# Attention with normalized queries and keys, then a gated feed-forward: repeats of the rest queries on VectorE or GpSimd, k and v of pairs 2 to 5 in runs of three tokens, score steps two at a time

## The chip, the cores and the metric

The kernel runs on one core of a Trainium2 chip. The metric is the device time of one execution in microseconds; before the change it is 424.69 (median of 3 runs, 423.41 to 424.93). The core has five engines with instruction queues of their own: TensorE (PE), VectorE (DVE), ScalarE (ACT), GpSimd (POOL) and SyncE (SP), and 16 DMA engines that serve the queues of SP, ACT and POOL.

## The reference

Eight batches of twelve heads, 448 tokens, 64 elements a head. Queries and keys are normalized, softmax attention is computed, the heads of a token are put side by side, and two matrix products with a gate between them follow.

```python
rms = np.sqrt(np.mean(x * x, axis=-1, keepdims=True) + 1e-06)   # for q and for k
...
scores = scale * np.matmul(q_n, k_n.transpose(0, 1, 3, 2))
attn = np.exp(scores - max); attn = attn / (sum(attn) + 1e-09)
x = np.matmul(attn, v).transpose(0, 2, 1, 3).reshape(3584, 768)
h = x @ w_in                                  # 768 x 2048
g = h * np.clip(h + 3.0, 0.0, 6.0) / 6.0
out = g @ w_out                               # 2048 x 768
```

## The kernel before

**Tiling.** Two heads make a pair; there are 48 pairs, six to a batch. The 448 tokens of a head are three full tiles of 128 and a rest of 64. A pair's work is: load k, q and v (`load_main`, `load_rest`), square (`square`, L403 on GpSimd or L401 on ScalarE), sum (`sums`, L406 on VectorE), the reciprocal root (`rstd`, L417 and L419 on ScalarE), normalize into bf16 (`normalize`, L427 and L429), turn tokens by elements into elements by tokens (`transposes` on TensorE up to pair 11, a DMA transpose from pair 12 on: `TD`), copy out of PSUM with the product of the two gains multiplied into the queries (`put_k`, and `put_q`, L465 on ScalarE or L467 on VectorE), four score steps (`score`, L476), four exponentials (`expo`, L492, or `expo_head`, L497), four weighings of v (`weigh`, L513), a division by the row sums (`divide`, L523 to L532), and a transpose back (`x_out`, L541 to L547, or a DMA).

**Score steps.** Step 0, 1 and 2 of a pair take one full tile of keys each, with two half-height matmuls (64 rows, one for each head) into two PSUM banks; step NT = 3 takes the rests of both heads in one full-height matmul. `steps(todo)` makes a chain of several steps that TensorE runs in a row. Pairs under `PB` go one step at a time, pairs up to `P3` two at a time, from `P3` on three at a time. Single and double steps write banks 0 and 1 (two halves each). A group of three puts its first step in banks 2 and 3 (`THIRD`), which the feed-forward uses otherwise, and its exponentials are those of L497. In the tile eR of a rest step `expo` writes 448 columns and, in a second small exponential, once more the last 64 at column 512 (`W4`), from where the weighing of the second head's rest reads them.

**Two orders of tokens.** The first `PD = MB = 6` pairs (batch 0) are dense: partition s of a half holds seven neighbouring tokens, so that q and k come in one run of 1792 bytes for each partition, with no separate rest; v comes in two transfers, one for each half of the partitions, with a rest of its own. Dense tiles are transposed in 64 x 64 pieces. Later pairs hold three neighbouring tokens on each of 128 partitions and load the rest of 64 tokens apart, beside zeros that `clear` writes. The weights arrive through GpSimd's queue in pieces (`W_IN`).

**Feed-forward.** `h_mm` (L561) makes 128 columns of h for a batch from six matmuls, `relu` (L567, ScalarE) and `gate` (L572, VectorE) make g, `y_mm` (L580) makes 128 tokens by 384 outputs from sixteen matmuls. They are the items of the lanes "h" and "y", take one of the banks that `FF` lists, and run on TensorE between the steps of the attention. Batch 0's first h column may begin when pair 4's output is there (`h_early`), the others when all six are.

**What sets the order.** The class `Plan` simulates the engines while the program is built, and writes the instructions out in the order that comes of it: `key` ranks an operation, `ways` lists the engines that may take it with an estimated duration, and the prices `FIRST` (up to 45 us) and `PRICE` (after it) weigh one engine against another. Every engine runs its instructions in the written order, so one that waits holds up all behind it. `hold(p)` puts a small write on GpSimd behind the normalization of pair p - 5 (p under 12) or p - `LA`; the loads of pair p wait for it. The product of the gains goes through `load_g`, `mix_g` (VectorE), `turn_g` (a matmul) and `put_g` (VectorE, L639). `DN` lists the normalizations that VectorE does (L427, of pairs 0 and 1), the others are GpSimd's.

## Time and profile before

| what | value |
|---|---|
| median of 3 runs | 424.69 us (423.41 to 424.93) |
| the profiled execution | 423.99 us, its span 422.1 us |
| granted TensorE clock over the span | 1.0 |
| ScalarE, VectorE, GpSimd busy | 291.7, 210.6, 201.3 us |
| moved by DMA | 65.12 MB, mean 154 GB/s |
| batch 0's last output transposes (pair 5) | from 39.23 us on TensorE |
| last exponential of the attention | ends before 320 us; GpSimd's last work before 300 us |

The page gives busy times of each engine, the chain of work that ended last, and groups of instructions by line. A view of windows gives the same for stretches of the span, the timeline lists instructions in order of their start, with the idle time before them and what ended it in brackets. On TensorE matmuls overlap: the duration of a row is longer than the step to the next start, and the distance of two starts is what a matmul costs. "x4" behind a row counts the instructions merged in it.

### The profile page before, as it was taken

Reading aid. Unit: us, or ns where it says so; the run is one execution under the profiler, and the core shown is the slowest. Engines: PE = TensorE matmul, PEld = TensorE weight load, DVE = VectorE, ACT = ScalarE, POOL = GpSimd, SP = SyncE. Lnnn points to the kernel's source line nnn. Section 1 sums busy time; section 2 is a strip of 40 time slices with the busy share of each in tenths; the row PEclk is TensorE's granted clock in tenths of the full one; section 3 lists DMA queues with packets and bytes.
Section 4 is the critical chain, followed back from the end, with each engine's and each line's share of the span. In section 5 each row is a group of like instructions: output and inputs, shape, how many; then the busy total and the mean of one; then the engine's idle time right before and its main releaser. Section 6 shows DMA issues by size and latency. Waiting matters only on the chain.

```text
span 422.1 us, 9498 instructions
## 1 busy us (share of the span) xinstructions
PE 406.6 (96%) x3692; PEld 237.1 (56%) x3692; DVE 210.6 (50%) x436; ACT 291.7 (69%) x713; POOL 201.3 (48%) x215
## 2 busy tenths in 40 slices
PE   2989999999999999999999999999999999999997
PEld 1565655455555555555555556565556555555565
DVE  7775978455444676457364664546243152042100
ACT  5899986766888988897869977789583243243211
POOL 5998956747676647756575676681000000000000
PEclk9999999999999999999999999999999999999999
DMA  8999899999998959988896968943420301100122
GB/s 253 252 217 235 155 235 176 198 244 176 189 246 208 245 109 201 233 195 202 158 248 168 248 122 198 255 106 77 76 64 13 88 0 39 75 2 37 76 75 76
DMA packets 124561, 65.12 MB, mean 154 GB/s; under 512 B 77412, under 2 KB 121060, under 8 KB 124516
## 3 DMA queue, kind: packets, MB, share of 16 engines
q1 hardware_dynamic: 116144, 57.76, 61.2%
q0 software_dynamic: 8080, 6.29, 10.2%
q8 instruction: 29, 0.48, 0.5%
q10 hardware_dynamic: 292, 0.46, 0.3%
q14 instruction: 16, 0.13, 0.1%
HBM read 45.61 MB, written 11.01 MB: 134 GB/s over the span
## 4 chain that ended last, share of the span: by engine, by line
PE 81%; ACT 5%; DMA 5%; issue 2%; DVE 2%; POOL 2%; SPq 1%; POOLq 0%; DVEq 0%; ACTq 0%
PE ps L580 34%; PE ps L561 29%; PE av L513 9%; PE sc L476 6%; DMA v_st<-in_v_dram 3%; ACT eD L492 3%; DMA qkT<-qkn 2%; PE ps L476 1%; DMA qk_st<-in_q_dram 1%; POOL qkn L429 1%; DVE ssq L406 1%; ACT t_sb L567 1%; PE ps L446 1%; SPq L376 1%; PE sc L561 1%
## 5 line engine op out<-in xcount | busy, mean ns | idle before, releaser
L561 PE MATMUL ps<-xT,w_in_sb 128*128 128x448 bf16 x750 | 165.4, 352 | 1.5 <-ACT eD L497 1.1
L580 PE MATMUL ps<-w_out_sb,gT 128*128 128x384 bf16 (+1 forms) x896 | 162.5, 323 | 0.0
L572 DVE SCALAR_TENSOR_TENSOR gT<-t_sb,ps 128x448 bf16<-128x448 f32 x125 | 76.9, 620 | 110.5 <-ACT t_sb L567 109.6
L492 ACT ACTIVATE eD<-sc 128x768 bf16<-128x768 f32 x240 | 113.3, 567 | 6.0 <-PE sc L476 5.6
L580 PEld LDWEIGHTS <-gT 128*128 128x128 bf16 x912 | 83.8, 98 | 57.2 <-issue 8.8
L561 PEld LDWEIGHTS <-w_in_sb 128*128 128x128 bf16 x768 | 69.8, 98 | 57.6 <-issue 6.1
L429 POOL TENSOR_TENSOR qkn<-qk_st,rstd 128x512 bf16<-128x512 f32 x84 | 85.2, 1043 | 25.0 <-ACT rstd L419 24.7
L403 POOL TENSOR_TENSOR sq<-qk_st 128x1024 f32<-128x1024 f32 (+2 forms) x50 | 81.6, 1642 | 31.8 <-DMA qk_st<-in_q_dram 18.5
L567 ACT ACTIVATE t_sb<-ps 128x448 f32<-128x448 f32 x125 | 69.8, 562 | 31.1 <-PE ps L561 28.5
L513 PEld LDWEIGHTS <-eD 128*128 128x128 bf16 x1152 | 52.4, 98 | 23.2 <-issue 6.3
L406 DVE TENSOR_REDUCE ssq<-sq 128x16 f32<-128x1024 f32 (+2 forms) x50 | 57.7, 1156 | 8.9 <-POOL sq L403 5.9
L379 ACT COPY y_sb<-ps 128x384 f32<-128x384 f32 (+1 forms) x43 | 20.6, 478 | 57.4 <-PE ps L580 57.3
L513 PE MATMUL av<-vaug,eD 128*128 128x65 bf16 x1152 | 58.9, 194 | 0.0
L476 PE MATMUL sc<-qkT 64*128 64x448 bf16 (+1 forms) x288 | 52.8, 358 | 3.2 <-DVE qkT L467 1.1
L379 POOL CAST vaug<-v_st 128x512 bf16<-128x512 f32 x29 | 17.7, 620 | 39.2 <-PE av L513 38.7
L497 ACT ACTIVATE eD<-ps 128x448 bf16<-128x448 f32 (+2 forms) x72 | 25.1, 419 | 15.7 <-PE ps L476 15.7
L492 ACT ACTIVATE eR<-sc 128x448 bf16<-128x448 f32 x96 | 32.9, 412 | 3.1 <-PE sc L476 2.9
L523 DVE RECIPROCAL rden<-av 128x7 f32<-128x7 f32 x48 | 9.7, 202 | 40.4 <-PE av L513 40.2
L476 PEld LDWEIGHTS <-qkT 64*128 64x128 bf16 (+1 forms) x336 | 15.4, 95 | 22.2 <-issue 14.5
L465 ACT ACTIVATE qkT<-qkT,gprime 128x448 bf16<-128x448 bf16 x36 | 24.8, 691 | 1.7 <-DMA qkT<-qkn 1.7
L529 DVE TENSOR_TENSOR xn<-av,rden 128x384 bf16<-128x384 f32 x42 | 23.4, 557 | 1.5
L513 PEld LDWEIGHTS <-eR 128*128 128x128 bf16 x240 | 16.7, 99 | 7.2 <-issue 1.9
(72 smaller groups left out, 177.8 us busy)
## 6 DMA issues: line engine op xcount, KB each, us to landing
qk_st<-in_k_dram SPq DMA_DIRECT2D x21, 384.0 KB, 4.0
qk_st<-in_q_dram SPq DMA_DIRECT2D x21, 384.0 KB, 5.5
v_st<-in_v_dram SPq DMA_DIRECT2D x21, 384.0 KB, 5.9
out_dram<-y_sb SPq DMA_DIRECT2D x20, 384.0 KB, 2.4
w_out_sb<-in_moe_w_out_dram POOLq DMA_DIRECT2D x4, 768.0 KB, 11.1
out_dram<-y_sb SPq DMA_DIRECT2D x15, 192.0 KB, 2.7
w_in_sb<-in_moe_w_in_dram POOLq DMA_DIRECT2D x3, 768.0 KB, 9.5
v_st<-in_v_dram SPq DMA_DIRECT2D x22, 64.0 KB, 5.7
```

The lines of the kernel that those rows point to most:

```text
L379: (eng.copy if eng is nc.scalar else eng.tensor_copy)(out=out, in_=in_)
L403: eng.tensor_tensor(out=sq, in0=x, in1=x, op=A_MULT)
L406: nc.vector.tensor_reduce(out=packed(p, ssq_r[:, p % NR, a]), in_=packed(p, sq_r[m % 2][:, a]), axis=mybir.AxisListType.X, op=A_ADD,)
L429: eng.tensor_tensor(out=qkn_r[p % NQ][:, a].rearrange("p t h d -> p h t d"), in0=qk_st[:, a, p % NS], in1=by[:, a].rearrange("p (h t) -> p ...
L476: nc.tensor.matmul(out=(bank(u[h]) if isinstance(u, tuple) else bank(u, h))[:, 0:S], lhsT=qkT[rows, 0, i * P:(i + 1) * P], rhs=qkT[rows, 1 ...
L492: nc.scalar.activation(out=out, in_=in_, func=EXP, bias=0.0, scale=1.0)
L497: nc.scalar.activation(out=e[:, c:c + cols.stop - cols.start], in_=src[:, cols], func=EXP, bias=0.0, scale=1.0)
L513: nc.tensor.matmul(out=av_ps[:, c:c + n], lhsT=e_part(p, i, h, j), rhs=va[:, i].rearrange("p h d -> p (h d)")[:, h * W:h * W + n], start=f ...
L561: nc.tensor.matmul(out=bank(m)[:, 0:S], lhsT=w_in_sb[:, kt, f * P:(f + 1) * P], rhs=xT[:, kt, b % NX, x_slot(b)], start=(kt == 0), stop=(k ...
L567: nc.scalar.activation(out=t[:], in_=bank(m)[:, 0:S], func=RELU, bias=0.5, scale=1.0 / 6.0,)
L572: nc.vector.scalar_tensor_tensor(out=gT[:, f, (b % 2) * S:(b % 2 + 1) * S], in0=t[:], scalar=1.0, in1=bank(m)[:, 0:S], op0=A_MIN, op1=A_MULT,)
L580: nc.tensor.matmul(out=bank(m)[:, 0:n], lhsT=gT[:, f, c0:c0 + P], rhs=w_out_sb[:, f, c:c + n], start=(f == 0), stop=(f == NFT - 1),)
```

## The change

- **Repeats.** The second, small exponential of a rest step goes. A new function `repeat` copies the 64 columns inside eR, on VectorE or GpSimd as the plan chooses.
- **Score steps.** `P3` becomes 48, so no group of three is left; `PB` becomes 10. The feed-forward's list of banks becomes (2,), (3,), (4,), with banks 0 and 1 added after the last score.
- **k and v of pairs 2 to 5.** A new constant `PK = 2` beside `PD = 6`: `is_dense(a, p)` is true for q up to pair 5, for k and v up to pair 1. k and v of pairs 2 to 5 come in runs of three tokens with rests apart; `clear` splits into `clear_k` and `clear_q`, and the unused eighth block of squares is cleared once.
- **Gains.** `mix_g` is a plain product on GpSimd and waits for the sums of pair 0 instead of its normalized values; the factor 1/8 moves into `unit`.
- **Pair 1.** `DN` keeps pair 0 alone, so pair 1 is normalized on GpSimd. The key of a normalization becomes (.., 4).
- **Constants.** Prices and estimates of the plan; `NQ` 4 for 5; `XQ` 4 for 6 (pairs whose output is packed in seven blocks and transposed by five matmuls); `TS` 6 for 12 (pairs from 6 on turn k and q into one bank); `LA` 4 for 3, with p - 4 for p under 10 in `hold`; `W_IN` in six pieces; the order of the first loads.

```diff
-    PRICE, FIRST, UNTIL = {"POOL": 0.5, "ACT": 1.5, "DVE": 1.5}, {"POOL": 0.5, "ACT": 1.7, "DVE": 1.0}, 45e3
+    PRICE, FIRST, UNTIL = {"POOL": 0.6, "ACT": 2.0, "DVE": 1.2}, {"POOL": 0.7, "ACT": 1.2, "DVE": 1.0}, 45e3
...
-    NV, NK, NX, NQ, NR = 4, 3, 3, 5, 4
+    NV, NK, NX, NQ, NR = 4, 3, 3, 4, 4
...
-    W_IN = 512, 256, 256, 512, 512
+    W_IN = 256, 256, 256, 256, 512, 512
...
-    TD, XD, XQ = 12, 12, 6
+    TD, XD, XQ = 12, 12, 4
...
-    DENSE, PD, MB = 2 * NT + 1, 6, 6
+    DENSE, PK, PD = 2 * NT + 1, 2, 6
...
+    def is_dense(a, p):
+
+        return p < (PK, PD, PK)[a]
...
-        if a < 2 and p < PD:
+        if a < 2 and is_dense(a, p):
...
-        if p < MB:
+        if is_dense(a, p):
             src = src.rearrange("h (s r) d -> s h (r d)", r=DENSE)
             for u, part in enumerate((lo, hi)):
...
+    def blocks(p, a):
+
+        return DENSE if all(is_dense(i, p) for i in range(a.start, a.stop)) else 8
...
         if i == NT:
             e, src = eR_t[:, p % NER], bank(u)
-            parts = (e[:, 0:S], src[:, 0:S]), (e[:, W4:W4 + REST], src[:, FULL:S])
+            parts = ((e[:, 0:S], src[:, 0:S]),)
...
+    def repeat(eng, p):
+
+        e = eR_t[:, p % NER]
+        eng.tensor_copy(out=e[:, W4:W4 + REST], in_=e[:, FULL:S])
...
-    def clear(eng, r):
+    def clear_k(eng, r):
         eng.memset(qk_st[REST:P, 0, r, 0, NT, :], 0.0)
         eng.memset(qk_st[0:REST, 0, r, 1, NT, :], 0.0)
+
+    def clear_q(eng, r):
         eng.memset(qk_st[REST:P, 1, r, :, NT, :], 0.0)
...
-        eng.memset(unit[:], 1.0)
+        for sq in sq_r:
+            eng.memset(sq[:, 1, DENSE:8], 0.0)
+        eng.memset(unit[:], 1.0 / 8.0)
...
-    def mix_g():
-
-        nc.vector.scalar_tensor_tensor(
-            out=g_two[:], in0=g_row[:, 0:1].to_broadcast([1, 2, D]), scalar=1.0 / 8.0,
-            in1=g_row[:, 1:2].to_broadcast([1, 2, D]), op0=A_MULT, op1=A_MULT,
-        )
+    def mix_g(eng):
+
+        eng.tensor_tensor(out=g_two[:], in0=g_row[:, 0:1].to_broadcast([1, 2, D]), in1=g_row[:, 1:2].to_broadcast([1, 2, D]), op=A_MULT)
...
-    SC, ANY = [(0,), (1,)], [(2,), (3,), (4,), (1,), (0,)]
+    SC, ANY = [(0,), (1,)], [(1,), (0,), (4,), (3,), (2,)]
...
-    FF = [(3,), (2,), (4,), (1,), (0,)], [(4,)]
+    FF = [(2,), (3,), (4,)], [(4,)]
...
-    W_AFTER, LA, VL = 2, 3, 1.2
-    DN = ((0, 0), (0, 1), (1, 0), (1, 1))
+    W_AFTER, LA, VL = 2, 4, 1.2
+    DN = ((0, 0), (0, 1))
...
-    V0, V2, LATER, AHEAD = 2.5, 0.8, -1, 2500
+    V0, V2, LATER, AHEAD = 2.5, 0.8, -1, 4000
...
-        held[p] = [add((-5, p), [("POOL", 80, lambda: nc.gpsimd.memset(cell, 0.0))], norms[p - (5 if p < 12 else LA)] + norms.get(p - NS, []))]
+        held[p] = [add((0, p), [("POOL", 80, lambda: nc.gpsimd.memset(cell, 0.0))], norms[p - (4 if p < 10 else LA)] + norms.get(p - NS, []))]
...
-    TS, WAIT = 12, True
+    TS, WAIT = 6, True
...
-            load(1, 1, 1, 0, 0, nc.scalar, "ACT")
-            lg = plan.dma((0.5, 1), 2, 40, lambda: load_g(nc.scalar), queue="ACT")
+            load(1, 1, 1, 0, 0, *Q1)
+            lg = plan.dma((0, 1.5), 2, 40, lambda: load_g(nc.scalar), queue="ACT")
...
-            load(0, 2, 2, 2 * (PD <= 2), 0)
-            load(1, 2, 2, 2 * (PD <= 2), 0)
-            load(2, 0, 2, 4, V0)
-            lv = load(2, 2, 2, 0, 2.5)
+            load(0, 2, 2, 4 * (PK <= 2), 0)
+            load(1, 2, 2, 0, 0)
+            load(2, 0, 2, 2, 2.0)
+            lv = load(2, 2, 2, 4, 0.3)
...
-            m1 = add((-3, 0), [("DVE", 450, mix_g)], [lg, *norms[0]])
+            m1 = add((-3, 0), [("POOL", 330, lambda: mix_g(G))], [lg, squares[0]])
...
-                    e = [add((p, 0), [("ACT", 850 if i < NT else 545, lambda p=p, i=i, c=cells[n]: expo(p, i, c["b"]))], [ops[n], old])]
+                    e = [add((p, 0), [("ACT", 850 if i < NT else 440, lambda p=p, i=i, c=cells[n]: expo(p, i, c["b"]))], [ops[n], old])]
                     (op.parts[n - 1] if third else op.gives).append(e[0])
+                    if i == NT:
+                        e.append(by((p, 0.5), 160, 100, lambda eng, p=p: repeat(eng, p), e))
...
-            PB, P3 = 8, 24
+            PB, P3 = 10, 48
```

More of the change, by code (lines that the diff above doesn't have):

```diff
@@ L204, in run @@
                     continue
-                if op.calm is not None and (self.backlog("SP", "ACT") > op.calm[0] + 0 or self.backlog("POOL") > op.calm[1]):
+                if op.calm is not None and (self.backlog("SP", "ACT") > op.calm[0] + 500 or self.backlog("POOL") > op.calm[1]):
                     continue
@@ L330, in bank16 @@
         return bank(u).bitcast(BF16)
[L332 removed]
+    plan = Plan(share=(2.0, 1.0, 0.45, 3.0, 0.42, 6.0, 0.4))
     add = plan.add
@@ L441, in transposes @@
     def transposes(p, b, which=range(2)):
-        for a in which if p < PD else ():
+        for a in (a for a in which if is_dense(a, p)):
             for t in range(DENSE):
@@ L449, in transposes @@
                 nc.tensor.transpose(bank16(b)[part, c0:c0 + D], none[part, :], identity[part, part])
-        for a in which if p >= PD else ():
+        for a in (a for a in which if not is_dense(a, p)):
             for t in range(4):
@@ L834, in stats @@
         else:
-            s2 = [add((st, 3), [("DVE", 1000 if p < PD else 1130, lambda: sums(p, both, m))], s1 + busy)]
+            s2 = [add((st, 3), [("DVE", 1000 if p < PK else 1130, lambda: sums(p, both, m))], s1 + busy + [zero])]
         squares.append(s2[-1])
```

103 lines of the change are left out of this document (55 added, 48 removed).

## The prediction

> **What bounds the kernel now.** I read the page first: engine times, then DMA queues.
>
> ```profile
> span 422.1 us, 9498 instructions
> PE 406.6 (96%) x3692; PEld 237.1 (56%) x3692; DVE 210.6 (50%) x436; ACT 291.7 (69%) x713; POOL 201.3 (48%) x215
> q1 hardware_dynamic: 116144, 57.76, 61.2%
> ```
>
> TensorE is the bound, with 15.5 us of the span idle. The execution took 423.99 us, so 1.9 us lie around its span; it is 0.7 us (0.16%) below the median of the runs, 424.69, and inside their spread. All sums below start from 423.99.
>
> Second, the view of windows: length, busy time and (count) of PE, PEld, DVE, ACT and POOL, granted clock, DMA share, GB/s.
>
> ```profile
> 20.00:36.00 16.00, 14.61 (x237) 9.69 (x236) 10.86 (x24) 15.70 (x44) 15.76 (x23) 1.00 1.12 230
> 80.00:160.00 80.00, 80.00 (x726) 44.63 (x725) 43.25 (x85) 64.66 (x152) 50.15 (x48) 1.00 1.03 206
> 160.00:320.00 160.00, 158.50 (x1494) 92.28 (x1493) 84.16 (x172) 132.01 (x337) 88.83 (x85) 1.00 0.77 165
> ```
>
> There are two regimes. From 20 to 36 us ScalarE (15.70 of 16.00) and GpSimd (15.76) are full, VectorE is not (10.86), and TensorE has only attention to do, since the feed-forward of batch 0 needs the outputs of its six pairs. There a microsecond taken from the leading chain moves everything after it. From 80 us on TensorE always has feed-forward matmuls beside the attention: no idle time from 80 to 160, where pairs are scored two steps at a time, and 160.00 - 158.50 = 1.5 us from 160 to 320, where most pairs are scored three at a time. There only matmul time and waits for a PSUM bank count; work taken from ScalarE is worth nothing by itself.
>
> **Score steps.** The chain of waits gives TensorE's undisturbed pace (start, length, line, count): 12.48 / 66 = 0.189 us for an input matmul, 8.78 / 54 = 0.163 for an output one.
>
> ```profile
> 324.57 8.78 PE ps L580 x54
> 333.34 12.48 PE ps L561 x66
> ```
>
> The timeline of TensorE then prices a group of steps:
>
> ```profile
> 105.22 0.73 PE L561 MATMUL ps<-xT,w_in_sb 128*128 128x448 bf16 x3
> 105.88 0.55 PE L476 MATMUL sc<-qkT 64*128 64x448 bf16 x4
> 106.37 0.42 PE L513 MATMUL av<-vaug,eD 128*128 128x65 bf16 x8
> ```
>
> ```profile
> 204.85 2.27 PE L580 MATMUL ps<-w_out_sb,gT 128*128 128x384 bf16 x13
> 207.05 0.36 PE L476 MATMUL ps<-qkT 64*128 64x448 bf16 x2
> 207.25 0.54 PE L476 MATMUL sc<-qkT 64*128 64x448 bf16 x4
> 207.73 0.34 PE L580 MATMUL ps<-w_out_sb,gT 128*128 128x384 bf16 x1
> ```
>
> ```profile
> 36.53 0.36 PE L476 MATMUL sc<-qkT 64*128 64x448 bf16 x2
> 36.82 0.36 PE L561 MATMUL ps<-xT,w_in_sb 128*128 128x448 bf16 x1
> ```
>
> Two steps cost 106.37 - 105.22 - 3 x 0.189 = 0.58 us, of which 105.88 - 105.22 - 0.57 = 0.09 is the entry from full-height matmuls. Three cost 207.73 - 204.85 - 13 x 0.163 = 0.77. One costs 36.82 - 36.53 plus that entry, 0.38 to 0.39. So pairs 24 to 47 pay 1.5 x 0.58 - 0.77 = 0.10 us each when triples go: **+2.4 us**. PB from 8 to 10 turns the three double groups of pairs 8 and 9 into six single ones: 6 x 0.39 - 3 x 0.58 = **+0.6 us**. Both lie in stages where TensorE is the bound, so nothing hides them.
>
> Against that stand the waits. A triple takes two of the three banks that the feed-forward asks for first, and the ends of the two largest waits between 160 and 320 us are:
>
> ```profile
> 185.18 1.11 PE L561 MATMUL ps<-xT,w_in_sb 128*128 128x448 bf16 x5 [0.85 <-ACT eD L497]
> 311.52 0.73 PE L561 MATMUL ps<-xT,w_in_sb 128*128 128x448 bf16 x3 [0.25 <-ACT eD L497]
> ```
>
> L497 is the exponential of a triple's first step, the one in the feed-forward's banks. Doubles use only banks 0 and 1, and the stage that runs on doubles (80 to 160) has no idle time. I take the whole 1.5 us as gone: **-1.5**; the ends are -1.5 and 0.
>
> **Output transposes.** XQ from 6 to 4 gives pairs 4 and 5 four transposes for five:
>
> ```profile
> 34.80 0.34 PE L544 MATMUL ps<-identity,xn 128*128 128x128 bf16 x3
> ...
> 35.22 0.41 PE L513 MATMUL av<-vaug,eR 128*128 128x130 bf16 x5
> ...
> 50.32 0.40 PE L541 MATMUL ps<-identity,xn 128*128 128x128 bf16 x4
> 50.55 0.40 PE L513 MATMUL av<-vaug,eR 128*128 128x130 bf16 x5
> ```
>
> (35.22 - 34.80) - (50.55 - 50.32) = 0.19 us each, **-0.4**. Their divisions become three VectorE operations for one, in a stage where VectorE has a third of its time free.
>
> **The start.** All engines, then ScalarE alone:
>
> ```profile
> 8.91 0.44 DVE L467 TENSOR_SCALAR qkT<-ps,gprime 128x448 bf16<-128x448 bf16 x1
> 9.07 1.82 POOL L403 TENSOR_TENSOR sq<-qk_st 128x448 f32<-128x448 f32 x2 [2.04 <-DVE ssq L406]
> 9.41 1.02 PE L476 MATMUL sc<-qkT 128*128 128x448 bf16 x3 [1.13 <-DVE qkT L467]
> ...
> 11.04 1.14 DVE L427 TENSOR_TENSOR qkn<-qk_st,ps 128x448 bf16<-128x448 f32 x2
> ```
>
> ```profile
> 13.93 0.98 ACT L492 ACTIVATE eD<-sc 128x768 bf16<-128x768 f32 x2 [0.23 <-PE sc L476]
> ...
> 15.97 0.66 ACT L492 ACTIVATE eR<-sc 128x448 bf16<-128x448 f32 x2 [0.60 <-PE sc L476]
> 16.52 0.64 ACT L465 ACTIVATE qkT<-ps,gprime 128x448 bf16<-128x448 bf16 x1
> ...
> 43.28 0.53 ACT L567 ACTIVATE t_sb<-ps 128x448 f32<-128x448 f32 x1
> 43.71 0.62 ACT L401 ACTIVATE sq<-qk_st 128x512 f32<-128x512 f32 x1
> ```
>
> First, the product of the gains leaves VectorE for GpSimd, which stands idle for 2.04 us before 9.07, and waits for pair 0's sums, no longer for its normalized values. Today pair 0's scaled queries start at 8.91 on VectorE and hold TensorE's first score back by 1.13 us. Gain 0 to 1.1; I take 0.5.
>
> Second, pair 1's normalizations go from VectorE, where they start at 11.04, to GpSimd in its gap; the planner's key puts them ahead of pair 2's squares (9.07). By GpSimd's 1.82 / 2 = 0.91 us for such a tile both can end by about 11, when today's first begins. ScalarE's two waits for scores there, 0.23 + 0.60 = 0.83, go with it. The other end is a loss: 1.8 us of work joins an engine that is full from 20 to 36 us, so pair 2 and its successors come later by up to 1.8 us. I take the gain, since TensorE's waits for GpSimd over the whole execution are these (line, whom for, total, times, longest):
>
> ```profile
> PE ps L446 <- POOL qkn L427: 0.2, 1, 0.2
> PE ps L453 <- POOL qkn L429: 0.2, 1, 0.2
> ```
>
>
> Third, the small exponential of each rest step. Both together hold ScalarE for 16.52 - 15.97 = 0.55 us, a tile of 448 columns alone for 43.71 - 43.28 = 0.43: 0.12 us each. Six pairs stand ahead of the feed-forward: 0.7 us. For the other 42 the saving is worth nothing, as ScalarE has 28 of 160 us free after 160. The repeats that replace them read 64 columns; they go to VectorE or GpSimd behind the whole exponential, and delay only the weighing of that rest step, which has feed-forward matmuls as cover; without that cover, 0.1 to 0.2 us each.
>
> Together **-2.0 us**, ends -2.6 and +1.8.
>
> k and v of pairs 2 to 5 in runs of three tokens change the loads: k's 128 runs a pair become 256 and 128 short ones for its rests, v's two half-height transfers one of the same runs. 4 x 256 = 1024 more packets at the page's mean for that queue (61.2% of 16 x 422.1 us over 116144 packets, 36 ns) are 2.3 us of the 16 engines, with the DMA share at 1.12. The cost lies between 0 and +2.3; I take 0, since the leading chain of the start waits for DMA only before 9 us, ahead of these tiles. The other edits of the start (clears split, transposes of pairs 6 to 11 into one bank, prices) shift work between engines without a price that a row shows.
>
> **Loads of later pairs.** The one long wait of the second stage:
>
> ```profile
> 78.91 0.35 PE L476 MATMUL sc<-qkT 128*128 128x448 bf16 x1 [0.82 <-ACT qkT L465]
> ```
>
> This is pair 12, the first through a DMA transpose. Its loads are held until a pair is normalized: pair 9 today (LA 3), pair 8 after (LA 4). The queue opens one pair earlier, and 0.8 us is a small part of that: **-0.8**. Loads of pairs 6 to 10 are held one pair longer (p - 4 for p - 5), so that the same wait could come back a little earlier: ends -0.8 and +0.8.
>
> The sum: +2.4 + 0.6 - 1.5 - 0.4 - 2.0 - 0.8 = -1.7, hence 423.99 - 1.7 = **422.3 us**.
>
> **The rivals.**
>
> (a) Doubles that are not paid for. The place is the score groups of pairs 24 to 47; the mechanism: the 1.5 us of waits are not the triples' banks but ScalarE or the gates running late (132.01 of 160 us busy), and doubles wait at banks 0 and 1 instead. Price +2.4 + 0.6 - 0.4 with the start's gain lost to the moved work: 423.99 + 2.6 = 426.6, slower. It decides from the point where start and waits together give less than 2.6. For it speaks that group costs are sure and gains are not; against it the idle-free 80 to 160.
>
> (b) The start gains more: first scores at the full 1.1 us earlier, and two of the three engines of the start, relieved by the new prices, bring batch 0's last pair 1.5 us nearer: 422.3 - 0.6 - 1.5 = 420.2. For it: VectorE's free third from 20 to 36 us. Against it: ScalarE gives up only 0.7 us.
>
> (c) The start becomes bound by GpSimd or the loads: +1.8 for the normalizations, or up to +2.3 for the packets, in place of -2.0: 422.3 + 2.0 + 1.8 = 426.1, with both 428.4. For it: GpSimd at 15.76 of 16.00, DMA share 1.12.
>
> (d) The repeats on VectorE collide with GpSimd, whose longest operation is
>
> ```profile
> L403 POOL TENSOR_TENSOR sq<-qk_st 128x1024 f32<-128x1024 f32 x36 | 67.7, 1894 | 27.4 <-DMA qk_st<-in_q_dram 16.9 <-issue 5.9 <-DVE rden L523 2.6
> ```
>
> Would a repeat have to stand behind one, the gates queued behind it on VectorE come up to 1.9 us late, and TensorE loses what the largest wait above cost, 0.85. At one repeat in ten, 5 x 0.85 = 4.3: 426.6. Against it: GpSimd is busy for 88.83 of 160 us, so half of the repeats meet nothing. The Trainium skill (SBUF — State Buffer, Who interferes with whom) speaks for this rival: a VectorE copy in a two-port mode and a GpSimd operation take one port pair in turn, and the later waits for the whole of the other. The trace of before has no such pair of operations in its later stages, so no row shows it.
>
> **How the numbers follow.** About 0.5% (2.1 us) is what a measurement of this kernel can tell from no change; against the median faster begins below 422.6, slower above 426.8. The forecast has 0.43 (own range 420.5 to 424.5: 0.24 faster, 0.19 same), (b) 0.18 (faster), (a) 0.19 (0.08 same, 0.11 slower), (c) 0.12 (0.03 and 0.09), (d) 0.08 (0.02 and 0.06). Faster 0.42, same 0.32, slower 0.26. The range leaves out the far ends of (b) and (c): 418.8 to 428.0.
>
> **What would show it.** Groups of L476 x6 gone, and no TensorE wait on an exponential from 80 to 320 us, or (a) is right. The first score near 8.9 us in place of 9.41, pair 1's qkn on GpSimd before 11, batch 0's last output transposes 2 us ahead of 39.2, or the start's gain is wrong; (c) shows as TensorE waiting for GpSimd's qkn. Repeats much longer than VectorE's other small operations, with gates late behind them, mean (d). The forecast fails as a whole if the planner's new prices reorder the start so that pair 0 itself comes later.

## The result and the profile after

The changed kernel takes **427.34 us** (median of 20 runs, 425.20 to 430.31), the kernel before on the same chips 424.62 (20 runs, 423.41 to 426.91): ratio **1.0061, interval 1.0046 to 1.0076**, 2.6 us slower. Once more in a later comparison: 426.98 (8 runs), 1.0051 (1.0028 to 1.0073). The execution profiled is one of the slower ones, 429.12 us; that of the later comparison took 428.00. Their spans are 5.1 and 4.0 us longer than the profiled one of before (427.2 and 426.1 against 422.1 us), where the medians differ by 2.7 and 2.4; so the losses read from these traces are larger than the median's. Small differences below are read with this spread in mind.

The page of after, engine times and queue:

```profile
span 427.2 us, 9420 instructions
PE 409.0 (96%) x3642; PEld 233.6 (55%) x3642; DVE 237.8 (56%) x492; ACT 269.7 (63%) x603; POOL 210.2 (49%) x252
q1 hardware_dynamic: 117312, 57.99, 60.8%
```

ScalarE lost 22 us of work, VectorE gained 27, and TensorE, which sets the end, gained 2.4. The windows of after (columns as before):

```profile
20.00:36.00 16.00, 12.98 (x202) 8.50 (x203) 13.94 (x29) 15.78 (x43) 15.65 (x20) 1.00 1.05 219
80.00:160.00 80.00, 80.00 (x708) 44.76 (x707) 47.57 (x93) 58.84 (x133) 51.20 (x52) 0.99 1.00 201
160.00:320.00 160.00, 160.00 (x1450) 88.19 (x1451) 90.82 (x180) 123.05 (x272) 96.82 (x110) 1.00 0.78 164
```

From 160 to 320 us TensorE has no idle time any more, as forecast. From 20 to 36 it fell from 14.61 to 12.98, and VectorE, which had a third of that time free, is now at 13.94 of 16.00: all three elementwise engines are close to full.

Busy time counts overlapping matmuls, so I split TensorE's time in another way. For each kind of neighbours the usual shortest distance of two starts is work, and what goes beyond it is lost. My sums from the matmul starts of the traces, in us:

```
                 work   lost 0-46  46-100  100-160  160-320  320-end
before          395.35   16.53      2.02    0.67     4.02     0.29
after           397.48   19.49      4.27    0.64     1.67     0.42
after, again    397.17   19.65      2.25    1.49     1.80     0.44
```

Work +2.1 (group costs), waits for banks -2.3, **the first 46 us +3.0**, where -2.0 was forecast, and 46 to 100 us +0.2 or +2.2. So the loss lies in the start. What TensorE waits for there (0 to 46 us; line, whom for, total, times, longest), before:

```profile
PE sc L476 <- ACT eD L492: 0.6, 3, 0.3
PE ps L446 <- POOL qkn L427: 0.2, 1, 0.2
```

and after:

```profile
PE sc L480 <- ACT eD L496: 3.4, 6, 1.1
PE ps L450 <- POOL qkn L431: 0.9, 1, 0.9
```

Most of what came new is waiting for ScalarE's exponentials. The first exponential of each pair (its rest step) starts at (us):

| pair | 0 | 1 | 2 | 3 | 4 | 5 |
|---|---|---|---|---|---|---|
| before | 9.97 | 15.97 | 19.99 | 23.53 | 27.59 | 31.65 |
| after | 11.53 | 15.81 | 21.86 | 25.28 | 29.28 | 33.27 |
| after, again | 11.64 | 15.91 | 21.96 | 25.39 | 29.39 | 33.38 |

Pair 0 begins 1.6 us late, pair 1 is on time again, pair 2 is 1.9 us late, and the pairs behind it stay late by about as much. The delay that lasts arises between pairs 1 and 2: 6.05 us for 4.02. Batch 0's last output transposes, which the prediction named as a mark of the start, come 0.9 us later (39.23 before) and not 2 us earlier:

```profile
40.12 0.39 PE L550 MATMUL ps<-identity,xn 128*128 128x128 bf16 x4
```

How pair 0 comes late shows in ScalarE's timeline of after:

```profile
8.60 0.63 ACT L406 ACTIVATE sq<-qk_st 128x512 f32<-128x512 f32 x1 [1.37 <-DMA qk_st<-in_k_dram]
9.14 0.19 ACT L421 ACTIVATE lnv<-ssq 128x7 f32<-128x7 f32 x1
...
11.05 0.58 ACT L406 ACTIVATE sq<-qk_st 128x448 f32<-128x448 f32 x1 [1.48 <-DMA qk_st<-in_q_dram]
11.53 0.53 ACT L496 ACTIVATE eR<-sc 128x448 bf16<-128x448 f32 x1
11.96 0.20 ACT L421 ACTIVATE lnv<-ssq 128x7 f32<-128x7 f32 x1
```

GpSimd's, with the same columns:

```profile
9.64 0.94 POOL L431 TENSOR_TENSOR qkn<-qk_st,rstd 128x448 bf16<-128x448 f32 x1 [3.09 <-ACT rstd L423]
...
12.47 0.93 POOL L431 TENSOR_TENSOR qkn<-qk_st,rstd 128x448 bf16<-128x448 f32 x1 [0.89 <-ACT rstd L423]
```

and TensorE's:

```profile
8.73 1.02 PE L480 MATMUL sc<-qkT 128*128 128x448 bf16 x3 [0.70 <-DVE qkT L471]
...
12.11 0.56 PE L480 MATMUL sc<-qkT 64*128 64x448 bf16 x2 [0.83 <-ACT eR L496]
```

The first score starts at 8.73 us (9.41 before), as forecast. But its exponential starts at 11.53 (before: 9.97), because both squares of pair 2 now stand ahead of it on ScalarE, and each waits for its load (before, q's alone stood there, at 9.38, and did not wait). Behind them wait also the roots of pair 1 (L421 at 9.14 and 11.96), for these GpSimd (3.09 and 0.89 us), and for ScalarE's exponential TensorE's next scores (0.83). Pair 1 is normalized at 13.4 instead of the forecast 11. The issues on SyncE's queue, before:

```profile
0.75 1.34 SPq L359 DMA_DIRECT2D qk_st<-in_k_dram  x3
2.14 0.47 SPq L359 DMA_DIRECT2D qk_st<-in_q_dram  x1
4.31 1.41 SPq L366 DMA_DIRECT2D v_st<-in_v_dram  x2
```

and after:

```profile
1.67 0.43 SPq L363 DMA_DIRECT2D qk_st<-in_q_dram  x1
2.14 0.43 SPq L372 DMA_DIRECT2D qk_st<-in_k_dram  x1
2.62 2.20 SPq L380 DMA_DIRECT2D qk_st<-in_k_dram  x2
4.87 0.61 SPq L363 DMA_DIRECT2D qk_st<-in_q_dram  x1
```

The k of pairs 2 and 3 is one load before and three after, its rests apart (L380). One more load stands ahead of them: q of pair 1 (1.67), which the kernel before issues on ScalarE's queue. In both traces the queue makes little headway from 2.6 us on: the next issue of before starts at 4.31, and the two rests take 2.20 us, where a run below that issues them from 4.32 us on needs 1.41. The q of pairs 2 and 3, issued at 2.14 before, comes behind all of these, at 4.87.

### The profile page after: what moved, and what is told of

It is laid out like the page before. It is cut to its first block, busy times and chain, and to the rows that moved or that the text cites. A ratio compares the mean times of both kernels' runs of the same rounds, so it can differ in the third digit from the quotient of the medians.

```text
span 427.2 us, 9420 instructions
## 1 busy us (share of the span) xinstructions
PE 409.0 (96%) x3642; PEld 233.6 (55%) x3642; DVE 237.8 (56%) x492; ACT 269.7 (63%) x603; POOL 210.2 (49%) x252
## 4 chain that ended last, share of the span: by engine, by line
PE 89%; ACT 5%; DMA 4%; issue 1%; DVE 1%; POOL 0%; SPq 0%; ACTq 0%
PE ps L589 35%; PE ps L570 33%; PE av L522 10%; PE sc L480 9%; ACT eD L496 3%; DMA qk_st<-in_q_dram 2%; DMA qkT<-qkn 1%; ACT eR L496 1%; ACT sq L406 0%; PE ps L457 0%; POOL qkn L433 0%; ACT rstd L423 0%; DVE ssq L412 0%; PE sc L550 0%; ACT lnv L421 0%
## 5 line engine op out<-in xcount | busy, mean ns | idle before, releaser
L570 PE MATMUL ps<-xT,w_in_sb 128*128 128x448 bf16 x768 | 173.9, 355 | 0.0
L589 PE MATMUL ps<-w_out_sb,gT 128*128 128x384 bf16 (+1 forms) x912 | 169.2, 323 | 0.0
L496 ACT ACTIVATE eD<-sc 128x768 bf16<-128x768 f32 (+1 forms) x288 | 135.9, 553 | 20.8 <-PE sc L480 18.2
L433 POOL TENSOR_TENSOR qkn<-qk_st,rstd 128x512 bf16<-128x512 f32 x88 | 89.9, 1040 | 28.7 <-ACT rstd L423 22.8
L408 POOL TENSOR_TENSOR sq<-qk_st 128x1024 f32<-128x1024 f32 (+2 forms) x47 | 78.6, 1683 | 12.8 <-DVE ssq L412 5.1
L480 PE MATMUL sc<-qkT 64*128 64x448 bf16 (+1 forms) x336 | 60.6, 362 | 6.9 <-ACT eD L496 3.4
L383 DVE COPY y_sb<-ps 128x384 f32<-128x384 f32 (+1 forms) x47 | 25.8, 549 | 70.5 <-PE ps L589 67.2
L412 DVE TENSOR_REDUCE ssq<-sq 128x16 f32<-128x1024 f32 (+1 forms) x50 | 58.0, 1165 | 4.4 <-ACT sq L406 2.6
L496 ACT ACTIVATE eR<-sc 128x448 bf16<-128x448 f32 x48 | 26.1, 545 | 10.9 <-PE sc L480 10.6
L469 ACT ACTIVATE qkT<-qkT,gprime 128x448 bf16<-128x448 bf16 x36 | 24.1, 676 | 2.4 <-DMA qkT<-qkn 2.4
L501 POOL COPY eR<-eR 128x64 bf16<-128x64 bf16 x32 | 7.5, 236 | 29.6 <-ACT eR L496 29.5
```

The costliest lines, as they stand in the source:

```text
L383: (eng.copy if eng is nc.scalar else eng.tensor_copy)(out=out, in_=in_)
L408: eng.tensor_tensor(out=sq, in0=x, in1=x, op=A_MULT)
L412: nc.vector.tensor_reduce(out=ssq_r[:, p % NR, a, 0:nb], in_=sq_r[m % 2][:, a, 0:nb], axis=mybir.AxisListType.X, op=A_ADD)
L433: eng.tensor_tensor(out=qkn_r[p % NQ][:, a].rearrange("p t h d -> p h t d"), in0=qk_st[:, a, p % NS], in1=by[:, a].rearrange("p (h t) -> p ...
L480: nc.tensor.matmul(out=(bank(u[h]) if isinstance(u, tuple) else bank(u, h))[:, 0:S], lhsT=qkT[rows, 0, i * P:(i + 1) * P], rhs=qkT[rows, 1 ...
L496: nc.scalar.activation(out=out, in_=in_, func=EXP, bias=0.0, scale=1.0)
```

## The experiments

The plan writes a new order for every price, so the first four runs, with one edit and planned again, also moved instructions that the edit does not name. In the runs named "written order kept" the order of the changed kernel (or of the kernel before) was taken as it stands, and only the edit moved. Times are medians; where nothing else is said the changed kernel's 427.34 and 426.98 are the neighbours to compare with, and the ratio is against the kernel before.

**Triples from pair 24 on**, planned again.

```diff
-            PB, P3 = 10, 48
+            PB, P3 = 10, 24
```

> The changed kernel with groups of three steps again from pair 24 on (P3 = 24). If the groups cost what the prediction took, 24 pairs get 0.10 us each back (2.4 us) and the waits for a PSUM bank between 160 and 320 us return (1.5 to 2.3 us): 426.4 to 427.2 against 427.3. Rival, that doubles cost nothing and only remove waits: 428.8 or more. In the trace: waits of TensorE on L501-type exponentials of a group's first step between 160 and 320 us.

430.64 us, 1.0141 (1.0114 to 1.0167), 3.3 us slower than the changed kernel where 0.1 to 0.9 faster was expected. Work fell by 1.8 us (395.72), near its price, but the loss from 160 to 320 us was 5.21 and behind it 2.33. TensorE's waits there (line, whom for, total, times, longest):

```profile
PE ps L480 <- DVE gT L581: 1.5, 3, 0.7
PE av L522 <- DVE xn L541: 0.8, 2, 0.4
```

Triples wait here for banks that VectorE's gates hold. That the time meets the number of the run's rival (428.8 or more) is no sign of it, since the work did fall. The feed-forward has three banks in this run, where the kernel before, with its triples, has five, so the run does not price the triples of before. What speaks against rival (a) is the changed kernel's own trace: its doubles wait for nothing from 160 to 320 us.

**q of pairs 2 and 3 ahead of k's rests**, planned again.

```diff
-            load(0, 2, 2, 4 * (PK <= 2), 0)
+            load(0, 2, 2, 0, 0)
...
+            load(0, 2, 0, 4, 0.5)
```

> The changed kernel with the load of q of pairs 2 and 3 put ahead of the two loads of k's rests on SP's queue, nothing else in the key order of the start. Theory (ScalarE stands behind the square of pair 2's q, which waits 1.48 us for its load, while pair 0's first exponential is ready at about 9.2): the first exponential of a rest step moves from 11.53 to between 9.9 and 10.5 us, and the time falls by 1.0 to 1.6, to 425.7 to 426.3. Rival (GpSimd, full from 20 to 36 us, sets the end of the start): the first exponential moves and the time stays at 427.3.

434.19 us, 1.0223 (1.0197 to 1.0248). The first exponential moved to 9.30, but the plan wrote another order, in which the engines of the start are not full:

```profile
20.00:36.00 16.00, 13.25 (x169) 8.29 (x167) 10.11 (x20) 11.79 (x27) 12.50 (x17) 1.00 1.12 210
```

TensorE also ran at half pace until 30.4 us in this execution (last section). This says nothing of the load, and much of how far one edit carries through the plan.

**Pair 2's squares on GpSimd only**, planned again.

```diff
-                 *[("DVE", ..., lambda a=a: square(V, p, one[a], m))] * (p < SQD)], ...)
+                 *[("DVE", ..., lambda a=a: square(V, p, one[a], m))] * (p < SQD)][:1 if p == 2 else 3], ...)
```

> The changed kernel with the squares of pair 2 allowed on GpSimd alone, so that ScalarE has no square that waits for a load ahead of pair 0's exponentials. Theory (ScalarE's wait is the loss of the start): first exponential of a rest step at 9.3 to 10.0 us, time 425.5 to 426.3. Rival (GpSimd sets the end of the start): two squares of 0.9 to 1.0 us more on GpSimd make it 428.2 or more.

433.91 us, 1.021 (1.0185 to 1.0235): first exponential at 9.68, and TensorE then waited 5.3 and 2.6 us for VectorE's divisions, with the half clock granted from 27.4 to 37.6 us. The plan again.

**k and v of pairs 2 to 5 dense again**, planned again.

```diff
-    DENSE, PK, PD = 2 * NT + 1, 2, 6
+    DENSE, PK, PD = 2 * NT + 1, 6, 6
```

> The changed kernel with k and v of pairs 2 to 5 dense as before (PK = 6), all else as changed. Theory (the loads of k's rests on SP's queue make q of pairs 2 and 3 late): start earlier by 1 to 1.5 us, 425.8 to 426.3. Rival (the runs of three tokens help, by v in one transfer): 427.5 to 428.5.

429.91 us, 1.0124 (1.0103 to 1.0145), slower than either forecast: first exponential at 9.16, pair 2's at 19.56 (21.86), and the least loss of these four runs from 10 to 20 us (3.67), then 5.45 lost from 46 to 80, where the half clock was granted from 58.4 to 61.8. The start is better at its head without the extra loads, and the plan of the rest is worse; no more can be read from it.

**q square of pair 2 behind the first exponential on ScalarE**, written order kept.

```diff
+ s = square(p=2, a=1); e = expo(p=0, i=0)
+ order: s directly behind e
```

> The changed kernel's written order kept instruction for instruction, but for one: on ScalarE the square of pair 2's q stands behind pair 0's first exponential instead of ahead of it. Theory (the loss of the start is that ScalarE waits 1.48 us for the load of that q): first exponential of a rest step at 9.3 to 9.8 us in place of 11.53, and 1.0 to 1.6 us off the time: 425.7 to 426.3. Rival (other work of the start, GpSimd or loads, ends last): the first exponential moves, the time stays within 0.4 of 427.3.

426.60 us, 1.005 (1.0026 to 1.0073). The first exponential starts at 9.76, 1.8 us earlier, that of pair 2 at 21.84 (21.86): the time is within the spread of the changed kernel.

**Both squares of pair 2 behind pair 0's first two exponentials**, written order kept.

```diff
+ s = square(p=2, a=0), square(p=2, a=1); e = expo(p=0, i=0)
+ order: both s behind e and the step that follows it
```

> The changed kernel's written order kept, but on ScalarE both squares of pair 2 stand behind pair 0's first two exponentials (the rest step and step 0), so that nothing of pair 0 and pair 1 stands behind a load of pair 2. Theory (the start is lost on ScalarE behind pair 2's loads; one square alone was not enough, since the queries' reciprocal root of pair 1 and step 0 still stood behind it): exponential of step 0 from 11.7 or 12.3 to about 10.5 us, pair 1's first exponential 0.5 to 1 us earlier, and 0.8 to 1.6 us off the time: 425.7 to 426.5. Rival (pair 2 is the next thing late, so that the gain is given back by pair 2's exponentials): 427.0 to 427.6.

427.78 us, 1.0072 (1.0047 to 1.0098). First exponential 9.30, pair 1's 16.09, pair 2's 22.34: all of it is given back. TensorE then waits 2.4 us for VectorE's copy of transposed tiles (L389). The rival was right: moving these squares on ScalarE only moves the loss.

**Three squares and two casts from ScalarE to VectorE**, written order kept.

```diff
+ square of pairs 3 to 5 on ACT -> DVE (3), cast_v of pairs up to 5 on ACT -> DVE (2)
```

> The changed kernel's written order kept, but the three squares of pairs 3 to 5 and the two casts of v of pairs 1 and 4 that ScalarE does are done by VectorE at the same places (2.6 us less on ScalarE before 30 us). Theory (ScalarE, full from 20 to 36 us, ends the start): pair 5's last exponential 1.5 to 2.5 us earlier, 425.0 to 425.8. Rival (GpSimd's normalizations or the loads end the start): the exponentials get gaps, and the time stays within 0.5 of 427.3; VectorE's squares, which read SBUF twice, could wait for GpSimd.

432.22 us, 1.0188 (1.0148 to 1.0228).

```profile
20.00:36.00 16.00, 11.37 (x135) 7.18 (x135) 14.24 (x24) 10.13 (x26) 12.34 (x15) 0.71 0.89 180
```

This is slower than either forecast. ScalarE falls to 10.13 us and VectorE is at 14.24. The five moved operations take 6.6 us on VectorE (the squares 1.51, 0.68 and 1.31, the casts 1.11 and 1.95) for 2.6 on ScalarE, and the granted clock of the window is 0.71: half from 23.5 to 30.3 and from 33.7 to 37.1 us. VectorE has no room for that much in the start; how much of the loss is the clock's stays open.

**Repeats back on ScalarE as second exponentials; the 16 repeats of VectorE to GpSimd; the latter with the two squares moved**, written order kept.

```diff
+ r_repact:  no repeat; expo(i=NT) writes 448 columns and then 64 at W4
+ r_reppool: repeat on DVE (16) -> POOL
+ r_comb:    r_kq2b and r_reppool together
```

> The changed kernel's written order kept, but the 64 columns of a rest step come from a second exponential on ScalarE right behind the first, as before the change, and the 48 repeats on VectorE and GpSimd are gone. Theory (the saving counts only at the start, about 0.12 us each for six or seven pairs, and the repeats held up behind GpSimd cost VectorE as much): within 0.8 of 427.3. Rival (repeats on VectorE that wait for GpSimd hold up the start): 1 us or more faster, 426.3 or less. Rival (ScalarE's relief is what the change lives on): 428.5 or more.

> The changed kernel's written order kept, but the 16 repeats that VectorE does are done by GpSimd at the same place of the order. Theory (VectorE's repeats take 0.17 us alone and up to 1.88 us while GpSimd works, but only the three before 36 us can move the end): 0 to 0.8 us faster, 426.5 to 427.3; VectorE loses 9.1 us of busy time. Rival (GpSimd is the bound of the start): slower by 0.3 or more.

> The changed kernel's written order kept with two edits together: both squares of pair 2 behind pair 0's first two exponentials, and the 16 repeats of VectorE given to GpSimd. Theory: the gains add, 0.6 for the repeats and 0.8 to 1.6: 425.1 to 425.9, still not below the kernel before (424.6). Rival (they are the same slack): not under 426.3.

427.51 us (1.0066, 1.004 to 1.0092), 426.69 (1.0044, 1.0022 to 1.0065) and 427.01 (1.0041, 1.0019 to 1.0063). Repeats against second exponentials: no difference that can be told. Off VectorE: 0.3 to 0.7 us below the changed kernel's two medians, inside the spread. The two edits together gain no more, as the rival said.

**The kernel before with its second exponentials as GpSimd copies**, written order kept.

```diff
+ expo(i=NT) writes 448 columns; tensor_copy on POOL half-way to the weighing, 48 times
```

> The kernel before with its written order kept, but the second exponential of each rest step is gone and GpSimd copies the 64 columns, at a place of the order halfway between the exponential and the weighing of the rest step. Theory (the saving on ScalarE counts at the start alone): 0.3 to 0.8 us faster than before, 423.8 to 424.3. Rival (a copy holds GpSimd up behind the exponential it reads, at 15.76 of 16 us busy): slower by 0.5 or more.

425.74 us against 424.69, 1.0033 (1.0009 to 1.0057): slower by 1.0, as the rival said, where 0.3 to 0.8 faster was the theory. ScalarE gives up 0.8 us from 20 to 36, and GpSimd, which now makes the copies too, stays where it was, full:

```profile
20.00:36.00 16.00, 13.89 (x245) 9.31 (x244) 10.81 (x25) 14.88 (x38) 15.76 (x26) 1.00 1.05 204
```

Of the 0.7 us that the prediction took for the small exponentials of the start nothing is left when GpSimd copies in their place, even in the old order. What leaving them out alone would give, no run shows.

**Pair 12 twelve matmuls later on TensorE**, written order kept.

```diff
+ put_q, scores, expo, weigh of p=12: 27.5 places later
```

> The changed kernel's written order kept, but pair 12's scaled queries, scores, exponentials, repeat and weighings stand behind twelve more input matmuls (2.3 us of TensorE). Theory (TensorE waits 1.86 us at 76.66 for the DMA transpose of pair 12 with feed-forward matmuls queued behind, and runs at half pace for some 2.5 us after it): no wait of over 0.3 us there, no matmuls at 0.37 us after it, and 2.5 to 3.2 us off the time: 424.1 to 424.8. Rival (the wait returns elsewhere, as ScalarE's exponentials of pair 12 come later): under 1 us gained, 426.4 or more.

428.21 us, 1.008 (1.0056 to 1.0104). From 46 to 80 us the loss falls to 0.50, from 80 to 160 it rises to 3.19:

```profile
PE sc L486 <- ACT eR L502: 1.2, 2, 0.7
PE av L528 <- ACT eD L502: 0.9, 1, 0.9
```

The wait moves on and is not removed; the rival was right.

**q of pairs 2 and 3 ahead of k's rests on the queue alone**, written order kept; then with the 16 repeats on GpSimd; and in the kernel before the same load put behind v's.

```diff
+ r_qload:  load_main(p=2, a=1) ahead of load_rest(p=2, a=0), on SyncE's queue only
+ r_qlrp:   the same and r_reppool
+ r_bqlate: before's order; load_main(p=2, a=1) behind v's loads of the first pairs
```

> The changed kernel with its written order kept on every engine; on SyncE's queue alone the load of q of pairs 2 and 3 is issued ahead of the two rest loads of k that the runs of three brought (2.20 us between the start of the one and the end of the other). If the loss of the start is the late landing of that q, the wait of 1.48 us of ScalarE's square of pair 2 goes, the first exponential starts at 10.0 to 10.4 us (11.53 before the edit), that of pair 2 at 20.5 to 20.9 (21.86), and the time is 425.7 to 426.4 us. If it is the order of work on ScalarE and GpSimd, or the k rests become the late load in its place (pair 2's other square needs them), the exponential of pair 2 stays at 21.7 or later and the time stays at 427.3 or so.

> The same edit, and the 16 repeats that VectorE makes are made by GpSimd. If both losses are real and add up, 425.0 to 425.8 us; by the rival for the load (nothing from it) 426.7 us, what the repeats alone gave.

> The kernel before with its written order kept on every engine; on SyncE's queue alone the load of q of pairs 2 and 3 (issued at 2.14 us) stands behind v's three loads of the first pairs, so it lands some 2 us later, as in the changed kernel. If that landing is what the start of the changed kernel lost by, the time rises by 1.0 to 1.5 us, to 425.7 to 426.2, with a wait for that load in the first 20 us; in the kernel before the squares of pair 2 stand on GpSimd, which has idle time there, so the rival says nothing is lost: 424.7 us.

427.00 us (1.004, 1.0007 to 1.0072), 427.57 (1.0057, 1.0025 to 1.009; 427.13 without its longest execution, 431.70) and 426.02 (1.0032, 1.0014 to 1.005). In the first run the first exponential moves to 10.35 and pair 2's to 21.19, and the time does not follow. The mirror met its forecast: with q issued at 6.34 us for 2.14 the kernel before takes 1.2 us longer. That q is 4.2 us late, the changed kernel's 2.7; and in the mirror's profile TensorE came to its full pace 3.5 us later than before (19.89 for 16.35), so for the changed kernel 1.2 is rather an upper bound. ScalarE of that run:

```profile
10.92 0.58 ACT L407 ACTIVATE sq<-qk_st 128x448 f32<-128x448 f32 x1 [1.42 <-DMA qk_st<-in_q_dram]
11.40 0.64 ACT L498 ACTIVATE eR<-sc 128x448 bf16<-128x448 f32 x2
```

But moving the load back in the changed kernel gained nothing that shows, so it was run once more beside the changed kernel on one chip.

> The changed kernel itself, once more, as the neighbour of the next run on one chip. 427 us, within 426.3 and 428.0; lost TensorE time in the first 46 us 18.5 to 19.6 us, with the first exponential between 10.1 and 11.6 us, as the loads land.

> The changed kernel with q of pairs 2 and 3 issued ahead of k's two rest loads, beside the changed kernel on the same chip. If the late landing of that q costs anything, it is 0.5 to 1.2 us below its neighbour; if k's rests, now later by 1.7 us on the queue, become the late load, it is within 0.4 us of it and the square of k waits 1.8 us or more where it waited 1.4.

426.98 us for the changed kernel, **428.92** (1.0094, 1.0057 to 1.0131) with the load moved. ScalarE of the latter:

```profile
9.42 0.63 ACT L412 ACTIVATE sq<-qk_st 128x512 f32<-128x512 f32 x1 [2.19 <-DMA qk_st<-in_k_dram]
9.96 0.19 ACT L427 ACTIVATE lnv<-ssq 128x7 f32<-128x7 f32 x1
...
10.30 0.56 ACT L412 ACTIVATE sq<-qk_st 128x448 f32<-128x448 f32 x1
10.76 0.52 ACT L502 ACTIVATE eR<-sc 128x448 bf16<-128x448 f32 x1
```

The wait for q is gone and the one for k has grown, from 1.59 us in its neighbour to 2.19. The rests are now the late load: whichever of the two comes second is late. That is the rival's sign. Its time, within 0.4 us of the neighbour, was not met: the start of this execution lost some 0.5 us less than the neighbour's (first exponential at 10.76 for 11.64), and what it lost more, 2.3 us, lies from 46 to 100 us, at pair 12 (last section). My theory that q's place alone is the loss is not borne out.

**Without the three squares between the exponentials of pairs 1 and 2**, written order kept.

```diff
+ square of pairs 3 to 5 on ACT: nothing (3)
```

> The changed kernel with its written order kept, and without the three squares that ScalarE makes between the exponentials of pairs 1 and 2 (two before the double step at 18.6 us, one at 20.18; 1.66 us of its time). Left out: the squares of k and q of three tiles of pairs 3 to 5; their sums are taken over what the buffer held, so these pairs are normalized by other numbers. If ScalarE's fullness sets the pace of the start, pair 2's first exponential comes 1.2 to 1.7 us earlier (4.4 to 4.9 us behind pair 1's, 6.1 with the squares) and the time falls to 425.3 to 426.2 us. If GpSimd's or VectorE's part or the loads set it, the exponential comes earlier and the next pairs do not, and the time is 427.0 or more.

427.25 us, 1.0064 (1.0042 to 1.0086). ScalarE:

```profile
16.38 0.54 ACT L502 ACTIVATE eR<-sc 128x448 bf16<-128x448 f32 x1
17.31 0.98 ACT L502 ACTIVATE eD<-sc 128x768 bf16<-128x768 f32 x2 [0.39 <-PE sc L486]
19.29 0.98 ACT L502 ACTIVATE eD<-sc 128x768 bf16<-128x768 f32 x2 [1.00 <-PE sc L486]
20.57 0.22 ACT L427 ACTIVATE lnv<-ssq 128x16 f32<-128x16 f32 x1 [0.30 <-DVE ssq L418]
...
22.36 0.53 ACT L502 ACTIVATE eR<-sc 128x448 bf16<-128x448 f32 x1
```

1.66 us of ScalarE's time less, and pair 2's exponential still comes 5.98 us behind pair 1's (6.05 with them, 4.02 in the kernel before). What was freed turned into waits for TensorE (1.00) and for VectorE's sums, behind which the roots stand, and behind these the exponential. VectorE in the same run:

```profile
19.33 1.21 DVE L418 TENSOR_REDUCE ssq<-sq 128x16 f32<-128x1024 f32 x1
...
20.76 2.33 DVE L418 TENSOR_REDUCE ssq<-sq 128x16 f32<-128x1024 f32 x2
```

So ScalarE's fullness by itself is not what holds the start either. One reservation: in this run the loads landed 0.6 us later and TensorE came to its full pace 3 us later than in the changed kernel (last section), so a gain of a few tenths could be covered.

## Why the prediction was wrong, step by step

**The failed step is the start**: "Together -2.0 us", made of three gains, and beside it "I take 0, since the leading chain of the start waits for DMA only before 9 us" for k and v in runs of three. Measured by lost TensorE time: +3.0 and +3.1 us in the two profiled executions, outside the range of this term, -2.6 to +1.8. The medians leave less: of their 2.4 to 2.7 us the other sums of the table take 0.1 to 0.8 where pair 12 costs 0.2, so an estimate for the start is +1.6 to +2.6, a loss where -2.0 was forecast, though it could lie inside the far end of the range.

- First score: 0.7 us earlier, 0.5 taken. Right in size, and worth nothing, as ScalarE was not ready for it.
- Pair 1 on GpSimd, 0.83: I counted GpSimd's free gap and not whom the tile waits for there. Its roots come from ScalarE, where they stand behind squares of pair 2 that wait for loads; GpSimd idled 3.09 and 0.89 us and ended at 13.4, not 11.
- Small exponentials, 0.7: nothing is left of it where GpSimd copies in their place, by the run in the old order.
- The loads: I looked where the leading chain waits today, not at what stands behind the new loads. A tile that was one load became three, on a queue that makes little headway from 2.6 to over 4 us, and the squares that wait for them stand ahead of the leading pair on ScalarE. That makes pair 0's first exponential 1.6 us late. The mirror run shows that a late load of this kind costs the kernel before up to 1.2 us. In the changed kernel, though, pair 1 is on time again, and the four runs that kept the order and brought pair 0's first exponential to between 9.3 and 10.8 us gained nothing that shows: pair 2's still came 6.05 to 6.25 us behind pair 1's. What a start without the extra loads, or with q of pair 1 back on ScalarE's queue, would give in the same order wasn't tried.
- What lasts is the stretch between pairs 1 and 2, 2.0 us longer than before. On ScalarE three squares (1.66 us) and a second pair of roots stand in it now. Leaving the squares out turned their time into waits for TensorE and for VectorE's sums. VectorE went from 10.86 to 13.94 us in the window from 20 to 36, with its sums ahead of the roots. That is read from the traces and supported by the run without squares, but no run made VectorE lighter there without moving something else, so the cause of these 2 us stays open between the order on ScalarE and VectorE's load.

**Group costs**, +2.4 + 0.6 - 0.4 = +2.6: work rose by 2.1, and fell by 1.8 when triples came back. Right, a little large.

**Waits for banks**, -1.5: measured -2.3 between 160 and 320 us, and no TensorE wait is left there. Right; I had counted waits alone and not the short distances that the triples also stretched.

**Pair 12**, -0.8: wrong, +0.6 to +1.0. The transposes did come earlier (the product of the gains, L469, at 75.94 for 78.19), but the plan put pair 12's first score earlier by more: TensorE was free for it at 74.80 us (76.66 - 1.86), for 78.09 before.

```profile
76.66 0.35 PE L480 MATMUL sc<-qkT 128*128 128x448 bf16 x1 [1.86 <-ACT qkT L469]
```

1.86 for 0.82 us, and 1.42 in the other execution. Putting it later only moved the wait.

**The rivals.** The time, 427.3, falls to (c), the start bound by GpSimd or the loads, 426.1 to 428.4 us. It got 0.12; its price rows (GpSimd at 15.76 of 16.00, DMA share 1.12) deserved more weight than the single waits that I collected as gains. Its mechanism came only in part: the sign that it named, TensorE waiting for GpSimd's qkn, is 0.9 us, and the waits for ScalarE's exponentials are the larger ones. (b) is out; (a) gives 426.6, near the time as well, but its doubles that wait at banks 0 and 1 are not in the trace. (d) happens as described but costs little (below). The far ends given for the whole range, 418.8 and 428.0, come out of none of the terms; (c) alone reaches 428.4.

The parts that were in the steady stages came out near their sizes and cancel: +2.1 - 2.3. What is left is the start.

## What to carry to other kernels

In a stage where several engines are full, the removal of a wait on one of them is no gain until it is followed through the in-order queues behind it: ask what else stands ahead of the leading instruction and what load that one waits for. A tile split into more loads has to be priced by what waits for the last of them, on whichever engine, and not by the chain that led before. Where a planner orders the work, test a single edit in a frozen order; a new plan for one constant cost up to 7 us here and hid the effect that was asked for.

## What the runs showed of the hardware

**A VectorE copy waits for a GpSimd operation.** The groups of after, shapes apart (busy us, mean ns):

```profile
L501 DVE COPY eR<-eR 128x64 bf16<-128x64 bf16 x16 | 9.1, 572 | 6.8 <-ACT eR L496 6.8
L501 POOL COPY eR<-eR 128x64 bf16<-128x64 bf16 x32 | 7.5, 236 | 29.6 <-ACT eR L496 29.5
```

The same copy takes 236 ns on GpSimd and between 170 and 1879 ns on VectorE. The longest one and what ran on GpSimd:

```profile
258.94 3.75 POOL L408 TENSOR_TENSOR sq<-qk_st 128x1024 f32<-128x1024 f32 x2
...
260.84 1.88 DVE L501 COPY eR<-eR 128x64 bf16<-128x64 bf16 x1
```

It starts 0.05 us after the second square of GpSimd (260.79 in the trace's records) and ends with it. The Trainium skill (SBUF — State Buffer, Who interferes with whom) has the rule: a VectorE copy in a two-port mode and a GpSimd operation lock one port pair against each other. This case agrees, with 0.17 us for an undisturbed copy and 1.88 for one that came behind a square. As the copies lie off the path, taking all sixteen away from VectorE gave 0.7 us at most, inside the spread.

**TensorE runs at half pace at first, and falls back to it after shorter idle times than expected.** At the start a pair of half-height scores takes 0.55 to 0.56 us in the traces, later 0.36. The change lies between 16.14 and 17.55 us in the changed kernel, between 13.33 and 16.38 before, and between 18.69 and 20.39 in the run without squares. The records of the granted clock begin inside these brackets, at 16.67, 16.35 and 19.73 us; a window without a record reads 1.00, so the 1.00 of the first windows does not mean full pace. From there on every change of the clock in a trace lies a multiple of 3.41 us behind the first record, and a stretch of half clock within a run lasts 3.41, 6.83 or 10.24 us. The Trainium skill (TensorE: Matmul & The Clock Gate, What's actually happening) speaks of an activity window of some 3.4 us that runs on its own and does not start with the kernel; the steps of 3.41 us and moments that differ by microseconds between executions agree with that.

Pair 12's wait shows the way back. In the changed kernel's profile it lasts 1.86 us, and the four input matmuls behind the next scores take

```profile
78.57 1.68 PE L570 MATMUL ps<-xT,w_in_sb 128*128 128x448 bf16 x4
```

The view of windows has the half clock there (recorded from 78.11 to 81.52 us):

```profile
79.00:80.00 1.00, 1.00 (x4) 0.37 (x3) 1.00 (x2) 0.74 (x4) 0.00 (x0) 0.50 1.82 225
```

In the later execution of the same kernel it lasts 1.42 us, and the same four take

```profile
76.33 0.35 PE L480 MATMUL sc<-qkT 128*128 128x448 bf16 x1 [1.42 <-ACT qkT L469]
...
78.04 0.93 PE L570 MATMUL ps<-xT,w_in_sb 128*128 128x448 bf16 x4
```

In eight traces with a wait there of 1.06 to 1.53 us all go on at full pace; of five with 1.85 to 2.42 us, four go on at half pace. The steps of the clock offer a reason why the fifth does not. In the changed kernel's profile steps fall at 74.70 and 78.11 us, and the wait, 74.80 to 76.66, lies whole between them; so it is in the other three. In the fifth (2.36 us, 75.30 to 77.66) a step at 76.01 cuts it, and no more than 1.66 us of it lie between two steps. So in these traces 1.85 us or more without a matmul between two steps was followed by the half clock, and 1.66 or less at this place was not; in the start of some runs, where TensorE has attention alone, 1.07 to 1.79 us were. This is read from the records, and no run tests it. That is most of the 2 us between the two executions of the changed kernel in the column from 46 to 100 us (4.27 and 2.25): a later landing of the transposed tiles is paid twice, as a longer wait and as the slower matmuls behind it. The idle time of over some 3.4 us that the Trainium skill (TensorE: Matmul & The Clock Gate, HAM oscillation — how this bites in real kernels) names is not needed here.
